# Attention and Fourier mixing on one core: new step lengths, delays, load flows and priorities for a list scheduler

## The chip, the cores and the metric

The kernel runs on one core of a Trainium2 chip. The metric is the device time of one execution in microseconds (us); the time before is the median of three runs. A core has five engines with queues of their own, each strictly in the order in which the program was written: TensorE (PE: matrix products, its weight loads are shown as PEld), VectorE (DVE), ScalarE (ACT), GpSimd (POOL) and SyncE (SP). [...] DMA transfers are issued here from the queues of SP and POOL.

## The reference, cut to what matters

Eight batches, 12 heads, 448 tokens, 64 values per head. Cosine attention first, then a real Fourier mix over tokens and features, a layer norm and a two-layer perceptron of 768, 3072 and 768:

```python
q_n = q / (norm(q) + 1e-6); k_n = k / (norm(k) + 1e-6)
attn = softmax(q_n @ k_n.T / tau)                # tau = 0.1
x = (attn @ v) laid out as [8, 448, 768]
u = x + real(fft(fft(x, axis=1), axis=2))
un = (u - mean(u)) / sqrt(var(u) + 1e-6)
out = u + relu(un @ w_ch1) @ w_ch2
```

## The kernel before, in words

The program is not written in the order in which it runs. `Kern.build` describes every piece of work as a *step* (`Plan.add`): the engines that may run it, a length for each, a priority, a name, and what it reads and writes. `Plan.schedule` then plays the machine through once, on the host while the kernel is built: at each turn it picks, per engine, the step that is ready first (the lower priority number on a tie; ACT and DVE may also wait a little for an urgent step), books it, and moves that engine's clock on. What comes out is nothing but an **order of steps in each of the five queues**, and for copies that ACT or DVE may do, which of them does it. `Plan.emit` writes the instructions in that order with semaphores for every dependency. Lengths and delays decide nothing but a step's place in its queue (and the number of filler groups, below).

Steps have names with a batch number behind the underscore. Those that matter here, with their lines:

- `ld_k`, `ld_q`, `ld_t` (SP) and `ld_v` (POOL, line 847) load queries, keys and values; `W1_n` and `W2_n` (POOL, lines 601 and 602) load twelve blocks of each weight matrix, one behind another three back.
- `sq`, `ss`, `ln`, `nrm`, `eps`, `rcp`, `sc`: squares (ACT, line 677 in batches 0 and 1, 806 later), sums over 64 values (DVE, line 679 or 808), logarithm and exponential for the square root (ACT, lines 620 and 622), reciprocal (DVE, lines 623 and 624), scaling (lines 704, 708 on DVE and POOL in batches 0 and 1, 815 on POOL later).
- Batches 0 and 1 are transposed on PE (`tk`, `tq`, `tt`, lines 732 to 757) and copied out of PSUM by ACT or DVE (line 723; `et` at 767). Batches 2 to 7 are transposed by DMA (`tr`), with two small copies behind it (`ktd`, `qdup`).
- `qk`: scores on PE, 64 rows of the array (line 889), and their tail with 128 rows (`qk?t`, lines 901 and 902). `ex`: exponentials on ACT (line 867). `pv`: values (lines 920 and 926). `rd`, `x`: division on DVE (lines 944 and 946).
- `fa`, `f0`, `f1`, `g` (DVE, lines 963 to 992), `fs` (PE, 1008 and 1013), `te` (1024, 1025), `fd` (PE, 1051), `qe`, `pq`, `u` (1064 to 1079): the two Fourier transforms by folded tables, and the sum u. `sind`, `sinp`, `sinn`, `half` (lines 568 to 586) make the tables while batch 0 runs.
- `ba`, `bs`, `ln2`, `rs`, `un` (lines 1111 to 1120): the layer norm. `tn` (1130) and `eu` (1138) turn batch 0's result; later batches use a DMA transpose (`tru`).
- `h` (line 1188, with `relu` at 1204) is the first product of the perceptron, `y` and `m` (line 1332) the second with its sums (1427) and results (1352 to 1364); for the last two batches `p` (line 1283) takes the place of `h`. These four form the **long stream** of products. Each of its steps depends on the one before (`self.main`), so the order inside the stream is fixed by the code. The scheduler decides only where attention steps of the next batch cut in.

Batch b+1's attention runs between batch b's stream. Before the first `h` (batch 0) there is no stream to fill PE. So `Plan.fill` puts groups of six products that nobody reads (line 1571) into PE's planned gaps of 0.4 us and more, up to the first `h` wherever they fit, later only where PE's planned use is below 0.75.

Priorities are a base (10 + 100 b for attention, 20 more for the Fourier part, 5000 + b for the stream, -1 for what empties PSUM), and a table, `SHIFT`, adds a number to single steps. Delays are constants: 0.11 us from a step to whoever waits for it, 0.2 from PE. `FLOW` has, by name, latency, service time and share of each DMA transfer, and `LATE` an extra reserve behind transfers. The loop at the heart, before:

```python
t = max(t, d.end + (SEM_LAT if d.eng != "pe" else PE_LAT) + (op.late if ... else op.margin if e == "pe" else 0.0))
...
d = op.durs[op.engs.index(e)]
...
op.start = t
free[e] = t + d
op.end = t + d
```

PSUM holds two slots of one bank for the stream and the transposes ("M") and three slots of two banks for attention and mixing ("G").

## Time and profile before

| | us |
|---|---|
| median of three runs (lowest, highest) | 578.48 (577.97, 578.67) |
| span of the profiled execution, first to last instruction | 576.7 |
| PE busy | 562.2 |
| DVE busy | 428.6 |
| ACT busy | 391.4 |
| POOL busy | 210.7 |
| start of the first `h` product | 51.49 |

The time of the profiled execution itself is not given beside its span; the median of the runs is 1.8 us above that span. "Busy" is the time with at least one instruction running. Matmuls overlap in the pipeline, and their ends are modelled: a single product takes some 0.16 us longer to come out than the next one waits to start. So two starts in the timeline, and not a duration, tell what a product costs. In the chain of waits each piece counts only from the end of the piece before, which is why pieces there are shorter than the same instructions in the timeline.

### The profile page before, as it was taken

Reading aid. Unit: us, or ns where it says so; the run is one execution under the profiler, and the core shown is the slowest. Engines: PE = TensorE matmul, PEld = TensorE weight load, DVE = VectorE, ACT = ScalarE, POOL = GpSimd, SP = SyncE. Lnnn points to the kernel's source line nnn. Section 1 sums busy time; section 2 is a strip of 40 time slices with the busy share of each in tenths; the row PEclk is TensorE's granted clock in tenths of the full one; section 3 lists DMA queues with packets and bytes.
Section 4 is the critical chain, followed back from the end, with each engine's and each line's share of the span. In section 5 each row is a group of like instructions: output and inputs, shape, how many; then the busy total and the mean of one; then the engine's idle time right before and its main releaser. Section 6 shows DMA issues by size and latency. Waiting matters only on the chain.

```text
span 576.7 us, 15950 instructions
## 1 busy us (share of the span) xinstructions
PE 562.2 (97%) x6496; PEld 443.3 (77%) x6496; DVE 428.6 (74%) x1066; ACT 391.4 (68%) x764; POOL 210.7 (37%) x323
## 2 busy tenths in 40 slices
PE   3999999999999999999999999999999999999998
PEld 3679888686687786978787687778878687969695
DVE  8879888887688778776768568765877587876363
ACT  8898885467975685687747676488737753848170
POOL 8525424543462525523270435413180120031303
PEclk9899999999999999999999999999999999999999
DMA  9999999892597729952594339932592110022001
GB/s 218 186 218 168 167 180 166 177 166 56 119 150 87 177 44 133 174 110 61 110 140 73 66 103 147 162 70 71 106 108 57 28 57 28 3 42 71 27 30 56
DMA packets 187834, 62.19 MB, mean 108 GB/s; under 512 B 166736, under 2 KB 185552, under 8 KB 187760
## 3 DMA queue, kind: packets, MB, share of 16 engines
q1 hardware_dynamic: 129792, 38.35, 35.2%
q0 software_dynamic: 57968, 22.81, 30.8%
q8 instruction: 51, 0.84, 0.6%
q14 instruction: 23, 0.19, 0.1%
HBM read 51.90 MB, written 11.01 MB: 109 GB/s over the span
## 4 chain that ended last, share of the span: by engine, by line
PE 94%; DVE 3%; POOL 2%; issue 1%; POOLq 0%
PE PS L1332 34%; PE PS L1188 31%; PE PS L1283 7%; PE PS L926 6%; PE PS L889 6%; PE PS L1013 2%; PE PS L920 2%; PE PS L1051 2%; PE PS L744 1%; PE PS L1571 1%; PE PS L901 1%; PE PS L902 1%; POOL VB L847 1%; DVE X L946 1%; DVE SM L679 1%
## 5 line engine op out<-in xcount | busy, mean ns | idle before, releaser
L1188 PE MATMUL PS<-UNT,W1b 128*128 128x256 bf16 (+1 forms) x1872 | 187.9, 256 | 0.0
L1188 PEld LDWEIGHTS PS<-UNT,W1b 128*128 128x128 bf16 x1872 | 156.2, 98 | 18.9 <-issue 4.3
L867 ACT ACTIVATE E<-PS 128x900 bf16<-128x900 f32 (+1 forms) x192 | 148.7, 828 | 27.8 <-PE PS L889 25.7
L1332 PE MATMUL PS<-W2b,HQ 128*128 128x384 bf16 x768 | 133.3, 326 | 0.0
L815 POOL TENSOR_TENSOR QH<-STG,SM 128x256 bf16<-128x256 f32 x126 | 79.1, 655 | 82.1 <-DVE SM L624 73.1
L1332 PEld LDWEIGHTS PS<-W2b,HQ 128*128 128x128 bf16 x768 | 73.9, 98 | 45.4 <-issue 0.9
L1357 POOL TENSOR_TENSOR OUTB<-OUTB,U 128x192 f32<-128x192 f32 x66 | 37.9, 594 | 163.6 <-ACT OUTB L1352 163.3
L1204 ACT ACTIVATE HQ<-PS 128x512 bf16<-128x512 f32 x83 | 49.6, 597 | 42.5 <-PE PS L1188 42.1
L1332 PE MATMUL PS<-TX,HQ 128*128 128x384 bf16 (+2 forms) x408 | 71.0, 321 | 0.0
L1427 DVE TENSOR_TENSOR HQ<-HQ 128x512 bf16<-128x512 bf16 x141 | 60.6, 456 | 13.8 <-ACT HQ L1204 7.7
L1332 PEld LDWEIGHTS PS<-TX,HQ 128*128 128x128 bf16 x408 | 38.4, 98 | 23.5 <-issue 1.1
L926 PE MATMUL PS<-VB,E 128*128 128x65 bf16 x1152 | 51.2, 193 | 0.0
L926 PEld LDWEIGHTS PS<-VB,E 128*128 128x128 bf16 x1152 | 47.6, 97 | 1.1
L806 ACT ACTIVATE QH<-STG 128x384 f32<-128x384 f32 x84 | 42.4, 521 | 7.8 <-DVE SM L808 7.1
L808 DVE TENSOR_REDUCE SM<-QH 128x6 f32<-128x384 f32 x84 | 44.2, 539 | 4.3 <-ACT QH L806 3.9
L1204 DVE TENSOR_SCALAR HQ<-PS 128x512 bf16<-128x512 f32 x43 | 29.7, 691 | 21.1 <-PE PS L1188 20.6
L1386 POOL DMA_INDIRECT out_dram<-OUTB,IDX x21 | 22.9, 1092 | 53.2 <-DVE OUTB L1364 36.4
L920 PE MATMUL PS<-VZ,E 128*128 128x130 bf16 x192 | 41.6, 219 | 0.3 <-DVE X L946 0.3
L889 PE MATMUL PS<-QK 64*128 64x225 bf16 x576 | 39.9, 260 | 0.2 <-ACT E L867 0.2
L1079 DVE SCALAR_TENSOR_TENSOR U<-ACG,X 128x384 bf16<-128x384 f32 (+3 forms) x70 | 39.4, 583 | 0.9
L1352 ACT ACTIVATE OUTB<-PS 128x384 f32<-128x384 f32 x33 | 16.2, 492 | 30.4 <-PE PS L1332 30.1
L946 DVE TENSOR_TENSOR X<-PS,RD 128x512 bf16<-128x512 f32 (+1 forms) x49 | 33.1, 678 | 1.2
(177 smaller groups left out, 795.5 us busy)
## 6 DMA issues: line engine op xcount, KB each, us to landing
STG<-in_k_dram SPq DMA_DIRECT2D x18, 384.0 KB, 4.1
STG<-in_q_dram SPq DMA_DIRECT2D x18, 384.0 KB, 3.8
VB<-in_v_dram POOLq DMA_DIRECT2D x24, 192.0 KB, 5.9
W1b<-in_moe_w_ch_dram POOLq DMA_DIRECT2D x12, 384.0 KB, 6.7
W2b<-in_moe_w_ch_dram POOLq DMA_DIRECT2D x12, 384.0 KB, 7.3
out_dram<-OUTB SPq DMA_DIRECT2D x7, 384.0 KB, 4.0
TX<-in_k_dram SPq DMA_DIRECT2D x2, 576.0 KB, 5.6
TX<-in_q_dram SPq DMA_DIRECT2D x2, 576.0 KB, 6.0
```

The lines of the kernel that those rows point to most:

```text
L806: P.add("act", lambda a, sq=sq, src=buf[:, w * x:w * x + w]: a.activation(sq, src, ACTF.Square), t_act(w), pr, f"sq{i}_{b}", reads=bn, wri ...
L808: P.add("dve", lambda v, o=SS[:, i, H // ns * x:H // ns * (x + 1)], sq=sq: v.tensor_reduce(o, sq.rearrange("p (h d) -> p h d", d=DH), AX.X ...
L815: r = v.tensor_tensor(v3(qh)[:, h:h + 4], v3(buf)[:, h:h + 4], RN[:, i, h:h + 4].unsqueeze(2).to_broadcast((128, 4, DH)), AluOp.mult)
L867: return a.activation(o, self.PS[:, bk:bk + nc_, 0:SQ2], ACTF.Exp, scale=1.0 / self.tau)
L889: i = pe.matmul(self.PS[:, bk + h, c0:c0 + NK], self.KT[r, jj, kt * 128:(kt + 1) * 128], self.QT[r, jj, cols], start=True, stop=True)
L920: r = pe.matmul(o, st(6), self.VZ[:, j, :], start=not split, stop=(split and i == 0), skip_group_check=True)
L926: r = pe.matmul(o[:, 65 * h:65 * h + 65], st(2 * kt + h), self.VB[:, kt, 2 * j + h, :], start=(split and i == h == kt == 0), stop=((not sp ...
L1188: r = pe.matmul(self.PS[:, bk, x * n:(x + 1) * n], self.W1b[:, j, ft * 128:(ft + 1) * 128], self.UNT[:, j, cs], start=(j == 0), stop=(j == ...
L1204: return e.activation(o, i, ACTF.Relu) if e is self.nc.scalar else e.tensor_relu(o, i)
L1283: r = pe.matmul(o[:, 128 * f:128 * f + 128], lhs(j, n * g + f), rhs[:, j, :], start=(start and j == 0 and f == 0), stop=(stop and j == 2 a ...
L1332: r = pe.matmul(self.PS[:, bk, 0:n], lhs(f), rhs(f), start=(start and f == 0), stop=(stop and f == NF // 2 - 1), skip_group_check=True)
L1427: P.add("dve", lambda v: v.tensor_tensor(cs(o), cs(a), cs(bq), op), 0.46, -0.5, f"{nm}{k}_{b}", reads=rd, writes=hr(o)(k))
```

## The change

The steps, their instructions and their dependencies stay. The following becomes different.

- Every step has two lengths from a table `TIMES` (by name and old length): how long until its result counts, and how long it holds its engine. Steps that the table lacks get a rule.
- The delay from a step to its reader is taken by engine, 0.036 to 0.037 us for PE, ACT and DVE and 0.1 for POOL, with 0.018 more when PE is the reader. The extra 0.16 of a product that comes out of PE now stands in its first length.
- `qk` steps (with their tails) are booked 0.095 longer on PE when they follow a step of the long stream.
- `FLOW` has new numbers; the reserves in `LATE` are cut in most places and raised for `h` (0.3 to 0.5).
- `SHIFT` is replaced as a whole: other steps, other numbers, among them for the first time many of the long stream (`h`, `m`, `p`).
- `fill` still asks for gaps of 0.4 us, measured against PE's planned ends, which now are the first of the two lengths.

```diff
-SEM_LAT = 0.11
-PE_LAT = 0.2
+SEM_LAT = {"pe": 0.037, "act": 0.036, "dve": 0.036, "pool": 0.1, "sp": 0.036}
+PE_IN = 0.018
+MODE = 0.095
...
-        r"tru\d_\d": (1.81, 1.0, 0.3), r"tr\d_\d": (1.72, 1.1, 0.38), r"sc_\d_\d": (1.7, 1.56, 0.6), r"st\d_\d": (1.54, 1.0, 1.5)}
+        r"tru\d_\d": (1.81, 1.0, 0.2), r"tr\d_\d": (1.99, 1.23, 0.43), r"sc_\d_\d": (2.12, 1.26, 0.41), r"st\d_\d": (1.26, 1.02, 1.5)}
+
+TIMES = {
+    "pe": {
...
+        "qk0.40": (0.368, 0.300), "qk0.59": (0.562, 0.495), "qk0.78": (0.757, 0.689), "qkt0.20": (0.358, 0.197), "tk0.33": (0.335, 0.174),
...
+        "et0.23": (0.265, 0.289), "et0.29": (0.324, 0.348), "eu0.46": (0.485, 0.371), "ex0.49": (0.546, 0.426), "ex0.83": (0.920, 0.801),
...
 SHIFT = {
-    "cst": {0: 101.5}, "iotad": {0: 116.2}, "vz0": {0: 497.7}, "ix4": {0: -4.5}, "vz1": {0: -249.7}, "pads": {0: 7.3}, "ldt1": {0: -555.5},
...
+    "iotad": {0: 12.9989}, "ktd0": {0: 91.8065}, "vz0": {0: -8.6883}, "vz1": {0: 2.448}, "pads": {0: 2.4458}, "half": {0: -127.0392},
+    "sinn": {0: 78.735}, "ldt": {0: 147.6096}, "ld_q0_0": {0: -17975121.1186}, "ld_t0_0": {0: -17975160.5301}, "sqK0_0": {0: -71.4629},
...
+    "ssT0_1": {0: -209.1662}, "scK0_1": {0: -147.7417}, "scQ0_1": {0: -87.617}, "scK1_1": {0: -147.8435}, "scQ1_1": {0: -78.79},
...
-LATE = {r"W[12]_\d+": 1.5, "tmd": 2.0, r"sq\d_2": 4.0, r"sq\d_\d": 2.0, r"sq[KQT]\d_1": 2.0, r"ktd\d": 3.0, r"qdup\d": 3.0, r"qk\d._[2-7]": 1.5, r"pv\d\d_[2-7]": 2.0, r"pv\d\d_1": 1.0, r"h\d+_[1-7]": 0.3}
+LATE = {r"W[12]_\d+": 1.5, "tmd": 2.0, r"sq\d_\d": 1.5, r"sq[KQT]\d_1": 1.5, r"ktd\d": 2.0, r"qdup\d": 2.0, r"qk\d._[2-7]": 1.5, r"pv\d\d_[2-7]": 1.5, r"pv\d\d_1": 1.0, r"h\d+_[1-7]": 0.5}
...
+        self.mode = 1 if re.match(r"[hymp]\d", name) else 2 if name[:2] == "qk" else 0
+        self.times = {e: self.time(e, d) for e, d in zip(engs, durs)}
+
+    def time(self, e, d):
+
+        key = re.sub(r"\d+", "", re.sub(r"_\d+$", "", self.name)) + f"{d:.2f}"
+        if key in TIMES.get(e, ()):
+            return TIMES[e][key]
+        return {"act": (d + 0.03, max(d - 0.07, 0.05)), "dve": (d + 0.05, max(d - 0.03, 0.05)), "pe": (d + 0.165, d)}.get(e, (d, d))
...
-                    t = max(t, d.end + (SEM_LAT if d.eng != "pe" else PE_LAT) + (op.late if d.dma is not None or d.eng == "pool" and op.late >= 1 else op.margin if e == "pe" else 0.0))
+                    t = max(t, d.end + SEM_LAT[d.eng] + (PE_IN if e == "pe" else 0.0) + (op.late if d.dma is not None or d.eng == "pool" and op.late >= 1 else op.margin if e == "pe" else 0.0))
...
-            d = op.durs[op.engs.index(e)]
+            lat, d = op.times[e]
...
+            if e == "pe":
+                d += MODE * (op.mode == 2 and last == 1)
+                last = op.mode
...
-            op.end = t + d
+            op.end = t + lat + d - op.times[e][1]
```

20 lines of the change are left out of this document (12 added, 8 removed), and 127 rows, old and new, of tables (SHIFT, TIMES).

## The prediction

> **What bounds the kernel now.** I read the page's head first, then the waits of TensorE (PE), then a table of stretches, and last the chain of waits in the start.
>
> ```profile
> span 576.7 us, 15950 instructions
> ## 1 busy us (share of the span) xinstructions
> PE 562.2 (97%) x6496; PEld 443.3 (77%) x6496; DVE 428.6 (74%) x1066; ACT 391.4 (68%) x764; POOL 210.7 (37%) x323
> ```
>
> PE is busy for 97% of the span, so the first question is where the other 3% lie, and whether "busy" hides waits. The waits of PE (engine, line, waited for: total us, times, longest):
>
> ```profile
> PE PS L1571 <- DVE UNT L542: 7.7, 1, 7.7
> PE PS L744 <- POOL TX L704: 0.8, 1, 0.8
> ```
>
> The long one is the wait for the first data. The next longest is 0.8 us, and the view lists none after batch 0's start that is longer. The table of stretches (us; busy time and count of PE, PEld, DVE, ACT, POOL; then granted clock, DMA share, GB/s):
>
> ```profile
> 10.00:20.00 10.00, 8.34 (x81) 6.20 (x79) 8.18 (x18) 8.17 (x16) 7.95 (x12) 0.83 1.64 144
> 16.00:18.00 2.00, 2.00 (x20) 1.44 (x18) 0.61 (x2) 0.93 (x3) 1.45 (x3) 0.50 0.87 35
> 20.00:30.00 10.00, 9.07 (x160) 6.79 (x159) 8.84 (x21) 9.67 (x16) 5.31 (x8) 1.00 1.28 253
> 30.00:40.00 10.00, 9.48 (x173) 7.66 (x170) 7.97 (x23) 9.79 (x13) 1.42 (x2) 1.00 1.30 232
> 40.00:50.00 10.00, 9.08 (x132) 8.44 (x130) 9.11 (x25) 8.98 (x18) 5.68 (x6) 1.00 1.09 138
> 60.00:100.00 40.00, 40.00 (x530) 33.44 (x528) 33.24 (x75) 30.86 (x55) 13.39 (x19) 1.00 1.32 170
> 100.00:200.00 100.00, 100.00 (x931) 73.78 (x929) 79.58 (x203) 69.44 (x149) 47.45 (x69) 1.00 0.77 133
> ```
>
> From 60 us on PE is busy in every stretch, with matmuls that the result needs, and at full clock. ACT (9.67 and 9.79 of 10) sets the pace from 20 to 40: it evaluates batch 0's exponentials (L867). Before 51.5 us, part of PE's busy time is filler (L1571). So two things bound the kernel: **how early the long stream of products starts, and PE's own work after that.** The order of that stream is fixed by a chain of dependencies in the code, which the change leaves alone. It can only be cut up differently by attention steps. The end of the chain of waits that leads to its first product (L1188):
>
> ```profile
> 40.46 1.26 DVE SM L679
> ...
> 43.86 1.01 PE PS L1571 x18
> ...
> 46.99 0.47 DVE QH L708
> ...
> 49.01 0.29 DVE QH L708
> ...
> 51.49 0.55 PE PS L1188 x7
> ```
>
> The three DVE pieces are batch 1's norms and scalings: the first of them reads OUTB, where the code keeps batch 1's squares,
>
> ```profile
> 40.38 1.34 DVE L679 TENSOR_REDUCE SM<-OUTB 128x18 f32<-128x1152 f32 x1
> ```
>
> and all three stand in VectorE's (DVE's) queue ahead of batch 0's mixing. They delay the start of the stream at 51.49.
>
> **The change, term by term.** No instruction is added or removed, except that the number of filler groups follows from the plan. What changes is the order in five queues, and on which of ACT and DVE some copies land. The span is 576.7, and 1.8 lie between it and the median of 578.48. I hold those 1.8 fixed and count against the median.
>
> **(a) Batch 1's steps inside batch 0's last chain.** They cost 1.26 + 0.47 + 0.29 = 2.02 us. The new lengths separate how long a step holds its engine from when its result is visible, so the plan sees this conflict better. Against it speaks the diff: it lifts several of batch 1's steps (`scK0_1` and `scK1_1` by 147.7 from a base of 110) above batch 0's, which have 10 to 32. So more of them may move forward. Bounds: +2.02 gained, or, if the second reduction (the 1.26 again) also lands on the chain, 1.26 lost. I take **1.3 gained**, near the row, less a third that comes back elsewhere.
>
> **(b) The slow stretch ahead of the first scores.** Between 15 and 18 us PE ran at half clock (0.50 in the row 16:18) and filler stands in its queue ahead of the first score products:
>
> ```profile
> 15.11 1.30 PE PS L1571 x12
> 16.41 0.64 PE PS L744 x3
> ```
>
> Eighteen such fillers took 1.01 us at 43.86, so twelve should take 0.67: 0.63 us lie in the way, and behind them waits the first of the exponentials that then fill ACT. Bounds: 0.63 gained, or as much lost if the new plan sets another such group there. I take **0.5 gained**.
>
> **(c) ACT's order in the first norm.** ScalarE's timeline:
>
> ```profile
> 9.27 0.31 ACT L620 ACTIVATE SM<-SM,MV 128x18 f32<-128x18 f32 x1
> 9.60 0.39 ACT L584 ACTIVATE CS<-CS 1x225 bf16<-1x225 bf16 x1
> 10.01 0.22 ACT L622 ACTIVATE SM<-SM 128x18 f32<-128x18 f32 x1
> ```
>
> A table step that nobody needs yet (L584) stands between the logarithm and the exponential of the first norm. It costs 0.39, and a gain of that much is the upper end. The lower end is a loss of the same size, from another table step in its place. The new list moves exactly this step (`half`) and the one behind it (`sinn`). I take **0.4 gained**.
>
> **(d) Cutting up the stream.** The new plan charges 0.095 us when a score step follows a product of the long stream, and nothing when it follows an attention product. PE's timeline shows both cases, first behind the stream, then behind L926:
>
> ```profile
> 256.66 0.38 PE L1188 MATMUL PS<-UNT,W1b 128*128 128x256 bf16 x2
> 256.97 0.76 PE L889 MATMUL PS<-QK 64*128 64x225 bf16 x12
> 257.66 1.48 PE L1188 MATMUL PS<-UNT,W1b 128*128 128x256 bf16 x12
> 258.98 0.26 PE L901 MATMUL PS<-QK,KTD 128*128 128x225 bf16 x1
> ```
>
> ```profile
> 84.45 0.34 PE L926 MATMUL PS<-VB,E 128*128 128x65 bf16 x6
> 84.64 0.22 PE L920 MATMUL PS<-VZ,E 128*128 128x130 bf16 x1
> 84.69 0.34 PE L926 MATMUL PS<-VB,E 128*128 128x65 bf16 x6
> 84.97 0.56 PE L889 MATMUL PS<-QK 64*128 64x225 bf16 x8
> 85.46 0.28 PE L1188 MATMUL PS<-UNT,W1b 128*128 128x256 bf16 x1
> ```
>
> Twelve L1188 of this shape take 258.98 - 257.66 = 1.32, so 0.11 each. The two from 256.66 are through by 256.88, and the score step starts at 256.97: 0.09 lost. Six L926 take 84.64 - 84.45 = 0.19. Those from 84.69 are through by 84.88, and the score step starts at 84.97: 0.09 lost again. So the entry costs the same behind either, and the plan's preference saves nothing. The way out costs too: eight take 0.49 and twelve 0.69, so 0.05 each, and 0.09 are left over. The tail step (L901), of full height, enters at no cost, but the plan charges it as well. After batch 0 the code makes 51 score steps (nine in each of three batches, six in each of four). On paper up to 51 x 0.095 = 4.8 us can be had here; by these rows none. Only two score steps with nothing between them save an exit and an entry, 0.18. Bounds: ten such pairs gain 1.8, ten fewer of those there are now lose 1.8. I take **nothing**, since PSUM slots rarely allow pairs.
>
> [...] By the plan's own rule the forecast would be up to 4.8 us lower.
>
> **Sum:** 1.3 + 0.5 + 0.4 = 2.2 gained; 578.5 - 2.2 = **576.3 us**. What is late next: the last block of the first weights.
>
> ```profile
> 50.69 0.82 POOL L601 DMA_DIRECT2D W1b<-in_moe_w_ch_dram  x1 [2.19 <-DMA W1b<-in_moe_w_ch_dram]
> ```
>
> It leaves at 50.69. Its queue, GpSimd's (POOL's), itself waited 2.19 for an earlier block, so a much earlier stream would run into its weights. The change moves these loads as well (`W1_1` by 143 instead of 0.4, `W1_3` no more by 369), past the value loads on the same queue, and SyncE's (SP's) loads and transposes with them; I see no row that tells the direction. This is why I don't take the full 2.02 + 0.63 + 0.39 = 3.0.
>
> **The rivals.**
>
> *Slower: reserves that were needed.* The new plan cuts the reserve it keeps behind transfers: 3 to 2 us before the copies that follow the transposes (`ktd`, `qdup`), 2 to 1.5 before squares and value products, 4 to 1.5 for batch 2's squares. Every queue is in order. A copy placed too early holds the evictions behind it, these hold PSUM slots, and PE stands.
>
> ```profile
> QK<-QH SPq DMA_TRANSPOSE x42, 3.7
> ```
>
> For it: a transpose takes 3.7 us from issue to landing as a median, so half take longer; and PE has no wait after the start today, so there a new plan can only lose. Against it: the measured flows are longer in part (1.72 to 1.99 for `tr`), so some of the reserve has moved into the lengths. Price: 1.0 us, the cut before `ktd`, in each of the six batches with transposes, 6.0 in all: 576.3 + 6.0 = **582.3**. It decides from 2.2 + 1.2 = 3.4 us on, or 0.57 per batch.
>
> *No change: the plan gains only on paper.* If the new priorities were chosen for term (d), they buy up to 4.8 us that isn't there, and (a) to (c) stay as they are or come back as other intrusions. For it: the diff moves many `h` and `m` steps by about 4600 to 4900, which lifts single products of the stream ahead of attention. Against it: the rows of (a) are plain, and the engine lengths are nearer to the trace. Price: 0 +- 1 us, **578.2**.
>
> *No change: a cold PE at the start of the stream.* Fillers are set into planned gaps of at least 0.4 us, and PE's planned ends now lie 0.16 later, so short gaps lose theirs. If PE idles before 51.49 as it did before 15, the stream starts at half clock. The row 16:18 shows the state, and 10:20 with 0.83 says how long it held: 0.17 of 10 us lost, at half clock, are 3.4 us. Price: half of 3.4, 1.7 us: **578.0**. [...]
>
> **How the numbers follow.** About 0.2% of 578.5, 1.2 us, is what a measurement of this kernel can tell from no change. Chances: forecast 0.55 (its own range 573.6 to 577.3: 3.0 and 1.8 gained at the lower end, 1.2 at the upper), slower by reserves 0.30, plan on paper 0.10, cold PE 0.05. Hence faster 0.55, same 0.15, slower 0.30. The range reaches from 573.0 (the lower end of the likeliest, less most of the 0.7 by which runs differ) to 582.5, the slower rival; some 0.06 lie below it and 0.12 above.
>
> **What would show it.** (a) right: no L679 or L708 in the chain ahead of the first L1188, and that product at about 49.3 instead of 51.49. (b): clock above 0.83 in 10 to 20, first L867 before 17. (c): L622 right behind L620. (d): a score step behind L926 still loses 0.09, and the time from the first L1188 to the end stays within 1 us of 576.7 - 51.5 = 525.2. The slower rival: PE waits after 60 us, for `KTD` copies or exponentials. I am wrong if the first L1188 isn't earlier by over a microsecond, or if the stretch behind it changes by over 2.

## The result and the profile after

The changed kernel takes **582.46 us** (median of four runs, 582.05 to 583.16) against 578.50 of the kernel before (four runs): a ratio of 1.0069, with a 95% interval of 1.0054 to 1.0083. It is 4.0 us slower, at the upper edge of the range, and on the other side than forecast. The profiled execution took 582.19, 1.8 above its span, the same distance as before. In the comparisons further down, 8 of 75 executions of the kernel before took 581.7 to 582.9 us as well, so a ratio there can differ from the quotient of the medians. Every line of the code stands 61 lower than before (L1188 is now L1249).

The page's head, after:

```profile
span 580.4 us, 15813 instructions
## 1 busy us (share of the span) xinstructions
PE 562.0 (97%) x6418; PEld 439.3 (76%) x6418; DVE 434.5 (75%) x1076; ACT 387.5 (67%) x754; POOL 216.1 (37%) x323
```

PE has 78 products fewer, thirteen groups of filler, and is busy as long as before. The span is 3.7 longer. The first product of the long stream says where to cut it: TensorE's timeline of after has it in the last of these rows.

```profile
42.87 0.85 PE L1632 MATMUL PS<-TX 128*128 128x128 bf16 x12 [1.15 <-DVE F L1031]
44.02 0.98 PE L1074 MATMUL PS<-CS,ACG 128*65 128x225 bf16 x8 [0.30 <-DVE ACG L1053]
...
51.08 0.51 PE L1191 MATMUL PS<-TX,F 128*128 128x128 bf16 x6 [0.18 <-DVE F L1181]
...
52.57 0.62 PE L1249 MATMUL PS<-UNT,W1b 128*128 128x128 bf16 x8 [0.35 <-ACT UNT L1199]
```

It starts at 52.57 instead of 51.49: **1.1 of the 3.7 are lost in the start**. The other **2.6 are lost in the stream** (527.8 from there to the end, 525.2 before). I counted them in PE's timeline. A wait is the time from the end of the last product (start plus count times the distance of two starts) to the next product. Waits over 0.25 us come to 3.5 in the stream of after, and before has none: where its useful products stand, at 57.2 and 496.1, it runs 24 products of filler, 1.3 in all, which after doesn't have. Smaller waits make up the other 0.4.

**The start.** The groups of ScalarE between 17 us and the last exponential (count, busy us, mean ns, idle time ahead of them and its releaser), before and then after:

```profile
L867 ACT ACTIVATE E<-PS 128x900 bf16<-128x900 f32 (+1 forms) x24 | 18.4, 832 | 0.2
```

```profile
L928 ACT ACTIVATE E<-PS 128x900 bf16<-128x900 f32 (+1 forms) x24 | 18.1, 837 | 2.2 <-PE PS L950 2.1
```

ACT sets the pace here. Before, it stood 0.2 us ahead of its 24 exponentials; now it stands 2.2, and 2.1 of them wait for scores, 0.6 of it ahead of the first. That first exponential is still 0.7 earlier (16.92 instead of 17.64), but the table load behind the last one is 1.2 later (38.17 instead of 37.01). Why the scores are late shows TensorE's timeline of after, with three transposes of the same shape at three times:

```profile
13.66 0.82 PE L805 MATMUL PS<-TX 128*128 128x128 bf16 x3 [0.31 <-DVE TX L765]
...
16.81 0.82 PE L805 MATMUL PS<-TX 128*128 128x128 bf16 x3
...
19.39 0.55 PE L805 MATMUL PS<-TX 128*128 128x128 bf16 x3
```

Less the 0.16 by which a product comes out later, three take 0.66 until about 19 us, and 0.39 then and 0.33 when warm (0.49 at 26.36). PE runs at half pace while it makes the first scores, as it did before; but before three such transposes were down to 0.54 at 18.29, and here only at 19.39. The table of stretches of after says otherwise:

```profile
10.00:20.00 10.00, 8.33 (x64) 5.40 (x63) 9.54 (x18) 8.37 (x17) 8.77 (x11) 1.00 2.46 151
16.00:18.00 2.00, 2.00 (x16) 1.16 (x15) 2.00 (x4) 1.25 (x2) 1.45 (x3) 1.00 2.97 90
...
60.00:100.00 40.00, 39.41 (x521) 32.35 (x519) 29.44 (x68) 32.19 (x58) 11.67 (x16) 1.00 1.07 156
```

A granted clock of 1.00 at half pace: the trace of after holds no record of the clock at all (its page has no row PEclk, that of before has one), and the column shows 1.00 where nothing is recorded. The lengths of equal products tell the pace here: from one start to the next, the 18 fillers at 19.84 in after take 0.056 each, and the 18 at 52.15 in `before_start` (below) 0.107.

Then two engines meet. VectorE's timeline at the end of batch 0's folding, and GpSimd's, both after:

```profile
41.40 1.75 DVE L1031 TENSOR_TENSOR F<-ACG 128x512 bf16<-128x512 bf16 x2
43.18 0.73 DVE L1584 COPY ACG<-F 128x8 bf16<-128x8 bf16 x1
```

```profile
41.66 2.21 POOL L642 TENSOR_SCALAR CS<-TX 128x770 bf16<-128x770 bf16 x1
```

Before, the same pair took 0.76, and GpSimd's step (`sinp`) began behind it:

```profile
39.70 0.76 DVE L970 TENSOR_TENSOR F<-ACG 128x512 bf16<-128x512 bf16 x2
```

The pair is 1.0 longer, and the copy of eight columns takes 0.73, where 0.19 do without GpSimd (`after_sinp`, below). PE waits 1.15 for the pair (the row at 42.87). The chain of waits behind it holds the batch-1 pieces of term (a):

```profile
43.92 1.10 DVE SM L740
...
45.66 1.72 DVE SM L740 x2
...
49.22 0.94 DVE QH L769 x2
```

They are not gone but longer, 3.76 instead of 2.02. Even so the fold product comes at 44.02 instead of 42.91, and the 8.55 from there to the stream are the 8.58 of before. In this stretch the chain of before shows 2.02 of filler (18 products, twice), but that is no saving of 2.02: behind each group the next product starts 0.2 later than the fillers' pace would have it (from 44.65 to 44.87, from 51.23 to 51.49), so the filler stood in waits that were there anyway. Nor is DVE the only engine with batch-1 work in the way. ScalarE's timeline of after, ahead of the first stream product at 52.57:

```profile
50.98 1.16 ACT L738 ACTIVATE OUTB<-W2b 128x1152 f32<-128x1152 f32 x1
52.03 0.48 ACT L1199 ACTIVATE UNT<-PS 128x384 bf16<-128x384 f32 x1
```

The copy (L1199) for which PE waits could start at 51.59, when the products of the row at 51.08 are out; a square of batch 1 (L738) holds it for 0.4.

**The stream.** TensorE's timeline at its four largest waits behind 53 us, and VectorE's ahead of the third:

```profile
58.61 1.51 PE L1249 MATMUL PS<-UNT,W1b 128*128 128x128 bf16 x24 [0.51 <-DVE TX L1265]
...
73.73 0.22 PE L981 MATMUL PS<-VZ,E 128*128 128x130 bf16 x1 [0.55 <-issue]
...
381.57 1.51 PE L1249 MATMUL PS<-UNT,W1b 128*128 128x128 bf16 x24 [0.57 <-DVE HQ L1265]
...
512.82 3.42 PE L1393 MATMUL PS<-TX,HQ 128*128 128x384 bf16 x20 [0.52 <-DVE HQ L1488]
```

```profile
380.23 0.56 DVE L1140 SCALAR_TENSOR_TENSOR U<-ACG,X 64x384 bf16<-64x384 f32 x1
...
380.83 0.69 DVE L1265 TENSOR_SCALAR HQ<-PS 128x512 bf16<-128x512 f32 x1
```

At 58 and 381 a mixing step (`u`) stands right ahead of the copy (`relu`) that empties the slot PE waits for. At 512 GpSimd is again at work beside DVE: a multiplication ahead of that wait (L1488, at 510.35) takes 0.79, and 0.42 at 377.61 where GpSimd rests. For the wait at 73.73 the profile names no releaser. The other three are no waits for a `KTD` copy or a transpose.

**Theories.** *Lengths*: an order is fitted to the lengths it is planned with. What these have wrong (a cold PE, `sinp` beside DVE, waits that aren't there) becomes gain on paper and loss on the chip. *Reserves*: the cut reserves behind transfers, the slower rival of the prediction. *Start*: all of it comes from the other order of the first 65 us. *Filler*: all of it comes from the fewer groups.

### The profile page after: what moved, and what is told of

It is laid out like the page before. It is cut to its first block, busy times and chain, and to the rows that moved or that the text cites. A ratio compares the mean times of both kernels' runs of the same rounds, so it can differ in the third digit from the quotient of the medians.

```text
span 580.4 us, 15813 instructions
## 1 busy us (share of the span) xinstructions
PE 562.0 (97%) x6418; PEld 439.3 (76%) x6418; DVE 434.5 (75%) x1076; ACT 387.5 (67%) x754; POOL 216.1 (37%) x323
## 4 chain that ended last, share of the span: by engine, by line
PE 86%; DVE 9%; ACT 2%; issue 1%; DMA 1%; SPq 0%; DVEq 0%; ACTq 0%
PE PS L1393 32%; PE PS L1249 27%; PE PS L1344 7%; PE PS L987 6%; PE PS L950 5%; DVE U L1140 3%; PE PS L981 2%; PE PS L1074 2%; PE PS L1112 1%; DMA TX<-in_k_dram 1%; ACT E L928 1%; PE PS L962 1%; PE PS L963 1%; PE PS L805 1%; DVE ACG L1128 1%
## 5 line engine op out<-in xcount | busy, mean ns | idle before, releaser
L1249 PE MATMUL PS<-UNT,W1b 128*128 128x256 bf16 (+1 forms) x1872 | 185.8, 256 | 1.6 <-DVE HQ L1265 0.6
L1249 PEld LDWEIGHTS PS<-UNT,W1b 128*128 128x128 bf16 x1872 | 156.6, 98 | 21.7 <-issue 4.3
L876 POOL TENSOR_TENSOR QH<-STG,SM 128x256 bf16<-128x256 f32 x126 | 83.2, 687 | 80.2 <-DVE SM L685 60.2
L1265 ACT ACTIVATE HQ<-PS 128x512 bf16<-128x512 f32 x88 | 52.5, 596 | 49.1 <-PE PS L1249 48.2
L1488 DVE TENSOR_TENSOR HQ<-HQ 128x512 bf16<-128x512 bf16 x141 | 62.2, 468 | 6.9 <-ACT HQ L1265 4.0
L987 PE MATMUL PS<-VB,E 128*128 128x65 bf16 x1152 | 51.1, 193 | 0.0
L987 PEld LDWEIGHTS PS<-VB,E 128*128 128x128 bf16 x1152 | 47.5, 97 | 1.5
L1140 DVE SCALAR_TENSOR_TENSOR U<-ACG,X 128x384 bf16<-128x384 f32 (+3 forms) x70 | 41.7, 615 | 0.8
L908 POOL DMA_DIRECT2D VB<-in_v_dram x24 | 25.6, 1074 | 43.3 <-PE PS L987 27.5
L1265 DVE TENSOR_SCALAR HQ<-PS 128x512 bf16<-128x512 f32 x38 | 26.2, 690 | 20.6 <-PE PS L1249 20.3
```

The source lines that it names most:

```text
L876: r = v.tensor_tensor(v3(qh)[:, h:h + 4], v3(buf)[:, h:h + 4], RN[:, i, h:h + 4].unsqueeze(2).to_broadcast((128, 4, DH)), AluOp.mult)
L987: r = pe.matmul(o[:, 65 * h:65 * h + 65], st(2 * kt + h), self.VB[:, kt, 2 * j + h, :], start=(split and i == h == kt == 0), stop=((not sp ...
L1140: return v.scalar_tensor_tensor(U[o0:o0 + n, ut, cs].rearrange("p (i e) -> p i e", e=2), src, 1.0, X[i0:i0 + n, x, cs].rearrange("p (i e) ...
L1249: r = pe.matmul(self.PS[:, bk, x * n:(x + 1) * n], self.W1b[:, j, ft * 128:(ft + 1) * 128], self.UNT[:, j, cs], start=(j == 0), stop=(j == ...
L1265: return e.activation(o, i, ACTF.Relu) if e is self.nc.scalar else e.tensor_relu(o, i)
L1488: P.add("dve", lambda v: v.tensor_tensor(cs(o), cs(a), cs(bq), op), 0.46, -0.5, f"{nm}{k}_{b}", reads=rd, writes=hr(o)(k))
```

## The experiments

In kernels with a pinned order a list of steps per queue takes the place of the scheduler's choice, so that only the lines of the diff move. `a_b: 2 -> 1` is the count of filler groups ahead of a step. All ratios are to the kernel before on the same chip.

| kernel | median us | ratio (95%) | first stream product | span less that |
|---|---|---|---|---|
| before | 578.50 | | 51.49 | 525.2 |
| after | 582.46 | 1.0069 (1.0054 to 1.0083) | 52.57 | 527.8 |
| old_start | 581.56 | 1.0028 (1.0006 to 1.0049) | 52.56 | 527.5 |
| new_start | 582.72 | 1.0065 (1.0048 to 1.0082) | 51.74 | 528.8 |
| old_order_new_fill | 580.23 | 1.0031 (1.0011 to 1.0052) | 51.61 | 527.1 |
| prio_only | 645.21 (one run) | | 55.58 | 587.8 |
| after_warm | 582.02 | 1.0061 (1.0048 to 1.0074) | 52.56 | 528.1 |
| after_sinp | 583.07 | 1.0074 (1.0061 to 1.0087) | 52.89 | 528.3 |
| after_evict | 583.80 | 1.0084 (1.0071 to 1.0097) | 53.99 | 528.3 |
| before_warm | 579.68 | 1.0014 (0.9997 to 1.0030) | 51.23 | 526.5 |
| after_dense | 584.21 | 1.0090 (1.0076 to 1.0103) | 52.68 | 530.3 |
| after_mended | 583.55 | 1.0083 (1.0070 to 1.0096) | 51.50 | 529.1 |
| before_start | 582.65 | 1.0059 (1.0046 to 1.0071) | 54.07 | 527.3 |
| after_fix | 582.43 | 1.0056 (1.0041 to 1.0072) | 51.61 | 530.2 |
| hand_84 | 588.41 | 1.0169 (1.0140 to 1.0197) | 56.45 | 530.6 |
| hand_002 | 583.16 | 1.0083 (1.0056 to 1.0110) | 53.51 | 527.9 |
| mode_010 | 584.11 | 1.0115 (1.0076 to 1.0153) | 53.07 | 528.5 |

The last two columns are of each profiled execution. The ratio is that of the comparison on one chip, not the quotient of the medians here.

### Half of the order each, the filler alone, the priorities alone

`old_start`: the queues of before up to 65 us of its plan, then those of after, filler by the new lengths.

```diff
-pe: tq0_0 tk0_0 tt0_0 tk2_0 qk00_0 tq1_0
+pe: tk0_0 tk1_0 tk2_0 tq0_0 tq1_0 qk00_0
...
```

> Every queue keeps the order of the kernel before until batch 0's first pass of up products is through (plan time 65), and has the order of the changed kernel from there. Measured so far: 578.5 before, 582.46 after; PE's useful work in the changed kernel is behind by about 1.0 us at 65 us, 2.2 at 100 and 3.0 at 200. Theory 'start' (the plan mis-sizes batch 0's steps, and what comes later pays for it): 1.0 to 2.2 us come back, 580.3 to 581.5, and the first stream product stands at 51.5 again. Rival 'reserves' (transfers and copies placed too tightly in the later batches): nothing comes back, 582.5 +- 0.6. Rival 'phantom price' (the plan buys 10 cheaper entries of score steps with waits elsewhere in the stream): nothing comes back either, 582.5 +- 0.6.

The time falls by 0.9 by the medians and by more by the ratios (1.0028 instead of 1.0069), but the stream starts at 52.56, no earlier than in after: with the new filler this order is cold too (a granted clock of 0.72 from 10 to 20, 0.83 before). TensorE's timeline shows a wait ahead of the slow products, 1.35 where the kernel before has 0.8, and then two waits of the stream that are those of after:

```profile
15.10 0.80 PE L992 MATMUL PS<-TX 128*128 128x128 bf16 x3 [1.35 <-POOL TX L952]
...
381.12 1.51 PE L1436 MATMUL PS<-UNT,W1b 128*128 128x128 bf16 x24 [0.57 <-DVE HQ L1452]
...
512.51 3.42 PE L1580 MATMUL PS<-TX,HQ 128*128 128x384 bf16 x20 [0.66 <-DVE HQ L1675]
```

So *start* isn't the whole, and the loss in the stream comes with the later order.

`new_start`: the mirror, after's order up to 65 us, then before's, filler by the old lengths (40 groups).

```diff
-pe: tk0_0 tk1_0 tk2_0 tq0_0 tq1_0 qk00_0
+pe: tq0_0 tk0_0 tt0_0 tk2_0 qk00_0 tq1_0
...
```

> The mirror image: the order of the changed kernel until the first up pass is through, then the order of the kernel before. Theory 'start': 1.0 to 2.2 us slower than before, 579.5 to 580.7, and first stream product near 52.6. Rivals 'reserves' and 'phantom price': the time of the kernel before, 578.5 +- 0.6. If old_start and new_start both lie near 582.5, the loss is in neither half but in how they meet.

With the old filler the order of after is warm at 13.5, and ACT stands 1.2 instead of 2.2 ahead of the exponentials:

```profile
L1056 ACT ACTIVATE E<-PS 128x900 bf16<-128x900 f32 (+1 forms) x24 | 17.9, 840 | 1.2 <-PE PS L1078 1.2
```

One of the two microseconds is the cold PE, the other the order itself. The stream starts at 51.74, 0.8 earlier than in after, though the collision is in it too (the pair takes 1.87). What it gains is lost at the seam: batch 1's steps come late for the older rest, and PE waits 2.3 in all from 60 to 76, this one the longest:

```profile
71.58 0.22 PE L1109 MATMUL PS<-VZ,E 128*128 128x130 bf16 x1 [0.63 <-issue]
```

Both mixes lie near 582, so the two halves don't split the loss between them: how the orders meet costs time as well.

`old_order_new_fill`: before's order pinned in all queues, the lengths, delays and flows of after, which here decide the filler alone: 29 groups instead of 37.

```diff
-SEM_LAT = 0.11
-PE_LAT = 0.2
+SEM_LAT = {"pe": 0.037, "act": 0.036, "dve": 0.036, "pool": 0.1, "sp": 0.036}
+PE_IN = 0.018
+MODE = 0.095
...
```

> Order of the kernel before on all five queues; only the filler of PE follows from the new lengths (29 groups in place of 37). Theory 'start' and both rivals: no effect, 578.5 +- 0.6. Theory 'filler' (fewer groups leave PE colder and the clock lower): slower by up to 1.7, the price that the prediction gave to half a stretch at half clock, 580.2, and a granted clock under 1.00 somewhere ahead of 51.5 where the kernel before has 1.00.

1.8 slower by the ratio, but not where *filler* has it: the start loses 0.1. The rest is lost in the stream. There 18 fillers now stand although PE has no gap (1.0), and a wait of 0.75 is new. TensorE's timeline:

```profile
93.77 1.46 PE L1582 MATMUL PS<-W2b,TX 128*128 128x384 bf16 x8 [0.75 <-issue]
...
103.72 1.17 PE L1824 MATMUL PS<-W1b 128*128 128x128 bf16 x18
```

The filler fills a gap that the old order has by the new lengths and not on the chip. That speaks for *lengths*. The wait isn't filler's doing: in this execution a square of ACT waits 2.56 for a load of keys (0.41 in the kernel before), and the copy that PE waits for comes behind it.

`prio_only`: the lengths, delays and flows of before, the priorities of after.

```diff
-SEM_LAT = {"pe": 0.037, "act": 0.036, "dve": 0.036, "pool": 0.1, "sp": 0.036}
-PE_IN = 0.018
-MODE = 0.095
+SEM_LAT = 0.11
+PE_LAT = 0.2
...
```

> The scheduler of the kernel before with its one length per step, and only the new list of priorities. The list was made for the new lengths. If priorities carry over by themselves, the time is that of one of the two kernels, 578 to 583. If a list fits only the lengths that it was made with, queues run into one another: I expect over 600.

645.21 us, a span of 643.4: 67 us more than the kernel before. But most of it is filler. The page:

```profile
L1577 PE MATMUL PS<-W1b 128*128 128x128 bf16 x1020 | 61.4, 219 | 0.2
```

With the old lengths the new list leaves gaps in the plan, and 170 groups of filler go into the stream: 1020 products at 0.056 are 57 of the 62.6 by which the stream is longer. How much of that covers waits that the chip would have shown, this run doesn't tell. So the list doesn't carry over to other lengths, but 67 us is not the price of its order alone.

### Mending after's start and its waits

`after_warm`: six more filler groups ahead of the first transposes.

```diff
-tq0_0: 7, tk0_0: 0, tk2_0: 0
+tq0_0: 9, tk0_0: 3, tk2_0: 1
```

> The changed kernel with all its orders, and 6 more groups of filler on PE ahead of batch 0's first transposes (9 in place of 7 ahead of the first one, 3 and 1 ahead of two later ones). In the changed kernel's trace PE runs at about 0.6 of its pace until 19.4 us (three products 0.82 us, 0.55 from there on), in new_start, with these groups, at full pace from 13.5 on. Theory 'cold start' (24 groups in place of 37 leave PE slow ahead of the scores): full pace from about 13.5, first product of the stream at 51.7 instead of 52.57, and 0.8 off the end, 581.6; if the chain behind gives some back, 581.6 to 582.3. Rival 'the start is set by the queues alone' (order): no effect, 582.46 +- 0.4.

PE is warm, ACT stands 1.2 only, and useful products are 1.4 ahead of after at 40 us. The collision and what follows it take it all. TensorE's timeline:

```profile
41.87 0.51 PE L1826 MATMUL PS<-TX 128*128 128x128 bf16 x6 [1.53 <-DVE F L1222]
...
43.17 1.71 PE L1265 MATMUL PS<-CS,ACG 128*65 128x225 bf16 x8
```

PE stands for 1.53 and, behind six fillers at full pace, for another 0.29; then eight products take 1.71 instead of 0.98 (the row at 44.02 of after): half pace again, and the clock record of this trace has it too, 0.5 from 42.81 to 46.22. The stream starts at 52.56, and the time is that of after.

`after_sinp`: GpSimd's step beside the pair (`sinp`) goes to DVE, behind the fold.

```diff
-pool: W1_6 W1_8 sinp W1_7
+pool: W1_6 W1_8 W1_7
-dve: g1_0:0 g1_0:1
+dve: g1_0:0 g1_0:1 sinp
```

> The changed kernel with one step moved: the sine table step that GpSimd computes from 41.66 to 43.9 us goes to DVE, behind the last of the fold's sums (g1). In the changed kernel the fold's pair of sums took 1.75 us beside it, 0.76 in the kernel before. Theory 'two engines slow each other': the pair takes 0.76 again, the step itself costs DVE 0.5 or so, the first product comes 0.5 earlier, 52.1, the end 581.9. Rival 'the pair was slow for another reason': it stays at 1.75, the first product comes 0.5 later, the end at 583.

VectorE's timeline:

```profile
42.28 0.76 DVE L1222 TENSOR_TENSOR F<-ACG 128x512 bf16<-128x512 bf16 x2
43.08 0.19 DVE L1775 COPY ACG<-F 128x8 bf16<-128x8 bf16 x1
...
43.57 0.52 DVE L833 TENSOR_SCALAR CS<-TX 128x770 bf16<-128x770 bf16 x1
```

The pair is back at 0.76 and the copy at 0.19, and the step that took GpSimd 2.21 takes DVE 0.52. That the collision is GpSimd's doing is shown. Yet PE stayed cold longer in this execution (ACT stood 3.0 ahead of the exponentials), the pair begins 0.9 later than in after, and the time is 0.6 above it. How the two hinder each other is not shown. In after the pair was done at 43.15, ahead of the end of GpSimd's step at 43.87 (GpSimd's ends are rough), so by these rows it didn't wait for the whole of that step.

`after_evict`: three copies out of PSUM ahead of the `u` steps, where three of the four waits stood.

```diff
-dve: u1_0:4 u1_0:2 relu8_0 | relu16_4:1 behind u1_5:5 | s21_6 behind s40_6
+dve: relu8_0 u1_0:4 u1_0:2 | relu16_4:1 behind u1_5:3 | s21_6 behind s22_6
```

> The changed kernel with three copies on DVE moved ahead of three mixing steps (u) that stand before them, where its trace shows PE waiting for those copies: at 58.6 (0.67 us), 381.6 (0.74) and 512.8 (0.68). Theory 'evictions behind u steps' (the u steps take 0.6 a piece where the table has 0.48): the three waits go, 2.1 in all, 580.4; if a product waits for the delayed u step instead, half of it, 581.4. Rival 'reserves': these waits only show what a late transfer left, others take their place, 582.46 +- 0.4.

The wait at 381 shrinks from 0.57 to 0.26 and the one at 512 is gone, so those were rightly read. The first moved copy gives 0.7 back from 60 to 70, and PE was cold until 22 in this execution: 18 fillers at 20 us took 2.08, and 1.17 in after with the same order. The start is 1.4 later, which no moved line explains.

`after_dense` and `after_mended`: filler groups that wait for DVE steps 1.6 us earlier and are more (38), alone, and with `sinp` on DVE and two of the three moved copies.

```diff
-tq0_0: 7, fs0_0: 2, fs1_0: 2, fd0_0: 2, tk0_1: 2, h0_0: 1
+tq0_0: 9, tk0_0: 3, tk2_0: 1, fs0_0: 3, fs1_0: 6, fd0_0: 3, tk0_1: 3, h0_0: 2
-new.deps.add([o for o in self.order["dve"] if o.end + 0.05 <= at + 0.1][-1])
+new.deps.add([o for o in self.order["dve"] if o.end + 0.05 <= at - 1.5][-1])
```

> The changed kernel with all its orders and 38 groups of filler in place of 24, in the start alone: as in after_warm, and 4 more ahead of the second fold's products (there after_warm stood 1.53 us, and its 8 products took 1.71 behind that, 0.98 in new_start), 1 more each ahead of the first fold, the mixing products, batch 1's first transpose and the stream. The fillers also wait for DVE steps that end 1.6 us earlier, so that none is held by a late one. Theory 'cold start': PE at full pace from 13.5 us to the stream without a break, 8 products in 0.98, first stream product at 51.6, end 0.9 earlier than the changed kernel, 581.5. Rival 'queues alone': first stream product between 52.3 and 52.6, end 582.0 to 582.5.

> after_dense with two more edits: the sine step on DVE in place of GpSimd (in after_sinp it freed the fold's pair of sums, 0.76 in place of 1.75), and the two late copies ahead of mixing steps (in after_evict the waits at 381 and 512 us went from 0.57 and 0.52 to 0.26 and 0). If all three count and nothing is given back: 0.9 + 0.5 + 0.8 = 2.2 below the changed kernel, 580.3. If the start has slack behind it (what PE gains ahead of the stream is lost at the first step of batch 1 that comes late): 0.8 + 0.3, 581.4.

`after_dense`: the early groups are through too soon, PE waits 2.2 behind them and is slow again (18 fillers in 1.76); the stream starts at 52.68. `after_mended` has the same steps and filler up to 40 us and waits 2.96 there, but PE stays at full pace (18 fillers in 1.17): between these two, part of the gain is the execution's and not the edit's. Its stream starts at 51.50, as in before, and useful products are 1.0 to 1.4 us ahead of after until 300 us. Then TensorE's timeline, and ScalarE's and the queue of SP with its transposes:

```profile
302.28 1.49 PE L1440 MATMUL PS<-UNT,W1b 128*128 128x256 bf16 x12 [0.54 <-ACT HQ L1456]
```

```profile
301.22 0.52 ACT L1058 ACTIVATE QH<-STG 128x384 f32<-128x384 f32 x1 [0.92 <-DMA QK<-QH]
```

```profile
293.58 6.12 SPq L1073 DMA_TRANSPOSE QK<-QH  x4
```

A square of a later batch waits 0.92 for a transpose; the copy behind it on ACT is late, and PE stands 0.54. In `after_dense` the same chain costs 1.43 at 304.44. In after the four transposes take 5.42 and nobody waits. This is the mechanism of *reserves*, real, but only 0.5 to 1.4 us, and only where other edits made PE earlier. After itself doesn't pay it.

`after_fix`: the filler, `sinp` on DVE, all three copies with the first on ACT, and that square later.

```diff
 (after_mended's edits; filler waits 1.6 earlier only behind 35 us)
-dve: u1_0:4 relu8_0 u1_0:2      act: relu12_3:1 sq0_6:1 sq6_5 (relu2_3:1 behind)
+act: bs1_0 relu8_0              act: sq0_6:1 relu2_3:1 sq6_5
```

> The changed kernel with its late steps put right one by one: the fillers of after_warm and after_dense (those ahead of 35 us timed as in after_warm), the sine step on DVE, the copies that PE waited for at 381 and 512 us ahead of mixing steps, the one at 58 us (relu8) moved from DVE, where it stands behind three mixing steps, to ACT, which has 1.2 and 0.7 us free there, and the square on ACT that waited for a transpose in after_mended and after_dense (at 300 us, 0.9 and 1.8) behind the copy that it held up. In the changed kernel PE's waits over 0.25 us from the first stream product on add up to 3.5 us, 0.5 in the kernel before. Theory 'late copies' (the stream loses its time in single waits for copies and exponentials that the plan puts too close): first stream product at 51.3 to 51.6, waits over 0.25 us at 1.5 or less, end 582.46 - 1.1 - 1.9 = 579.5. Rival 'given back' (each repair lets PE run into the next late step): waits stay at 3 or more, end 582 to 584, as after_mended.

The stream starts at 51.61 and the mended waits are gone (0.26 is left behind 381), but others of the same size stand elsewhere. TensorE's timeline, the two largest:

```profile
59.43 0.50 PE L997 MATMUL PS<-TX 128*128 128x128 bf16 x3 [0.72 <-DVE TX L957]
...
304.37 0.98 PE L1266 MATMUL PS<-CS,ACG 128*65 128x225 bf16 x8 [0.92 <-DVE ACG L1245]
```

582.43, after's time: 1.0 gained in the start is given back in the stream, as *given back* has it. (Counted from start to start, the kernel before has no wait over 0.25 us in its stream, not 0.5.) No mended version beats the kernel before.

### The prediction's terms on the kernel before

`before_warm`: term (b) alone; the filler ahead of the first scores goes to earlier places.

```diff
-tq1_0: 2, tk2_0: 1, tq0_0: 0
+tq1_0: 0, tk2_0: 2, tq0_0: 2
```

> Term (b) of the prediction alone, on the kernel before: the 12 fillers ahead of the second query transpose go, 18 more stand in the gap ahead of the first one, where PE waits 0.8 us for GpSimd. All orders are those of the kernel before. By term (b): full pace from 14.6 on, first scores at 16.4 instead of 17.04, first stream product 0.5 earlier (51.0), end 0.5 earlier, 578.2 beside 578.7. Rival 'the exponentials take their pace from elsewhere': first scores earlier, but first stream product within 0.2 of 51.49 and the end unchanged. Rival 'the start has slack': the stream starts 0.5 earlier, and PE waits that much later on, at 496 or before; end unchanged.

Everything is 0.61 earlier up to the fold, just what the term said. Then VectorE's and GpSimd's timelines:

```profile
41.03 1.80 DVE L1185 TENSOR_TENSOR ACG<-F 128x256 bf16<-128x256 bf16 x2
```

```profile
41.80 2.21 POOL L774 TENSOR_SCALAR CS<-TX 128x770 bf16<-128x770 bf16 x1
```

GpSimd's step stands behind a load in its queue and comes at 41.80 instead of 42.51, as much earlier as DVE: this pair takes 1.80, where it took 1.12 before. The 1.12 seem not to be free of it either. VectorE's timeline of before, and of `before_start`, where DVE does that step:

```profile
41.64 1.12 DVE L992 TENSOR_TENSOR ACG<-F 128x256 bf16<-128x256 bf16 x2
```

```profile
40.90 0.51 DVE L1246 TENSOR_TENSOR ACG<-F 128x256 bf16<-128x256 bf16 x2
```

So the kernel before probably paid 0.6 already, though GpSimd's step is shown to begin late in the pair (its times are rough). The fold product comes at 42.88 instead of 42.91. The ratio can't be told from 1.

`before_start`: terms (a) and (c); batch 1's reductions and scalings behind batch 0's mixing, batch 0's steps ahead on ACT, `sinp` on DVE.

```diff
-dve: f11_0 ssK0_1 ... scK1_1 scK2_1 un0_0
+dve: g1_0:1 sinp te1_0:1 ssK0_1 u0_0:0 u0_0:1 ... un0_0 scK1_1 scK2_1
-pool: W1_8 sinp
-pe: fd1_0:0 tk0_1 fd1_0:1 tk1_1 tk2_1 tn0_0
+pe: fd1_0:0 fd1_0:1 tk0_1 tn0_0 tk1_1 ... h3_0 tk2_1
-act: sind gc1_0 ... sqT0_1 te0_0 te1_0 ... ek1_1 ek2_1 eu00_0 eu01_0
+act: sind te0_0 gc1_0 te1_0 ... rs0_0 eu00_0 eu01_0 ... ek1_1 ek2_1
```

> The kernel before with batch 0's last chain cleared as terms (a) and (c) of the prediction wanted it: on DVE the first reduction of batch 1's squares (1.26 us at 40.46) goes behind the copy that follows the second fold, two scalings of 0.47 behind the normalisation of the first tile, and the sine step comes to DVE behind the fold's sums; on ACT the two copies of the mixed keys and the small copy stand ahead of the table load (1.28) in place of behind it; three transposes of batch 1 on PE and their copies stand later. By the prediction's step (a): first stream product 1.3 to 2.0 earlier than 51.49, end 1.3 to 2.0 earlier, 576.8 to 577.5. Rival 'given back': first stream product 1 to 2 earlier, but batch 1's steps, now later, hold PE after 55 us for as long, end 578.5 to 579.5. Rival 'another gate': the mixing products wait for something else, first stream product within 0.5 of 51.49.

The fold product is 0.43 earlier and the mixing 0.57. Then ACT is the gate, in the chain of waits:

```profile
46.25 1.05 ACT W2b L931
47.30 1.05 ACT OUTB L931
```

Two squares of batch 1 stand ahead of batch 0's normalisation on ACT. PE waits 1.85 for it, the next products run at half pace (18 fillers in 2.13), and the stream starts at 54.07. So the 2.02 of term (a) are not to be had from DVE alone: another engine with batch-1 work is late next.

### Are the lengths it? Other numbers, planned anew

If one length is short, another number should let the plan come true. `hand_84` plans with a longer delay into PE, `hand_002` and `mode_010` with nearly the same numbers.

```diff
-PE_IN = 0.018
+PE_IN = 0.084
```

```diff
-PE_IN = 0.018
+PE_IN = 0.020
```

```diff
-MODE = 0.095
+MODE = 0.100
```

> The changed kernel with one number changed: the planner reckons 0.084 us in place of 0.018 for PE to take up work that another engine hands over, so 0.12 per hand-over in all, about what the kernel before reckoned (0.11); the planner orders all five queues anew by it. Its plan ends at 582.5 us, that of the changed kernel at 575.2 (measured span 580.4, so 5.2 later than planned), that of the kernel before at 582.1 (576.7, 5.4 earlier than planned). Theory 'reserve' (the waits of the stream come from hand-overs planned without reserve): PE's waits over 0.25 us from the first stream product on fall from 3.5 to 1 or less, and the span lies near the plan or below, 579 to 583, time 581 to 585. Rival 'lengths' (each step is late by its own error, reserve or not): waits stay at 3 or more, span 5 above the plan, time near 589.

> As hand_84, with 0.020 in place of 0.018: next to no change of the lengths, but the planner orders anew; plan end 575.9. Theory 'picked by the plan' (the list of priorities was chosen for the end of its own plan, so that plan ends too early by what the model leaves out, 5.2 us): span 581.1 +- 1, time 582.9 +- 1. If a chance order is as good as the picked one by the chip, but not by the plan, the time lies within 1 of 582.5 as well, and the planned end says nothing about the last 1%.

> As hand_002, with the price of a score step behind the stream at 0.100 in place of 0.095 and the hand-over as in the changed kernel; plan end 577.0. Theory 'picked by the plan': span 582.2 +- 1, time 584 +- 1. The start, which the plan leaves as it was, gives the same first stream product as the changed kernel, 52.6 +- 0.4, and PE's waits over 0.25 us in the stream lie at 3 or more again.

(`hand_84` doesn't compute the reference's result, and why is open. All its products run; its time is that of an order that can't be used.)

The spans are 587.0, 581.4 and 581.6 where the scheduler's own ends are 582.5, 575.9 and 577.0: later by 4.5, 5.5 and 4.6, and 4.0 to 4.4 of it are lost before the stream starts. A longer delay into PE only adds its own time (waits over 0.25 us in the stream are 5.9 instead of 3.5), so what is missing isn't a delay of this kind. The change of 0.002 us moves 34 steps of the first three batches, and the profiled execution starts its stream 0.9 later than after; that of 0.005 moves 577 steps, none of them of batch 0. The medians are 0.7 and 1.7 above after's, the first no clear difference. The bands of *picked by the plan* hold both spans, but for `hand_002` its alternative holds as well, so that is not decided; `hand_84` came out as *lengths* had it.

What the kernel's scheduler books for the two orders (filler takes no time in it) stands beside the chip's spans so:

| order | lengths | stream starts | stream lasts | end |
|---|---|---|---|---|
| before's | old, on paper | 52.6 | 529.5 | 582.1 |
| before's | new, on paper | 49.9 | 531.5 | 581.4 |
| before's | chip | 51.5 | 525.2 | 576.7 |
| after's | new, on paper | 48.7 | 526.4 | 575.1 |
| after's | chip | 52.6 | 527.8 | 580.4 |

By its own lengths the change gains 6.2 us, 1.2 in the start and 5.1 in the stream. The chip gives -1.1 and -2.6. In the old order's stream the new lengths book 3.6 us of waits over 0.25 us, of which the chip shows none in the kernel before (filler of 1.3 covers two places). The new order has 0.6 of them on paper, and 3.5 on the chip. So the new priorities **avoid waits that weren't there, and buy for it waits that the lengths don't show**. The start is too short on paper for both orders, by 1.6 for the old and by 3.9 for the new.

## Why the prediction was wrong

**The sum** missed by 6.2 us (576.3, and 582.46): it had 2.2 gained ahead of the stream, where 1.1 were lost, and nothing behind its first product, where 2.6 were lost. **The bound** was rightly named: how early the stream starts, and PE's own work after that. Both tests that I set for being wrong came true: the first stream product is later, not earlier by a microsecond, and the stretch behind it is 2.6 longer.

**(a), 1.3 gained: wrong sign.** The step that failed reads "I take 1.3 gained, near the row". The batch-1 pieces on the chain grew from 2.02 to 3.76. I had the evidence against me (the diff lifts `scK0_1` and `scK1_1`), and gave it no weight against a plain row. And the 2.02 were no free money: `before_start` shows ACT's batch-1 squares as the next gate. I counted the path to the stream on DVE, without asking what ACT still had to do; in after, too, a batch-1 square stands ahead of ACT's last copy.

**(b), 0.5 gained: no gain.** The filler ahead of the first scores cost what I said, as `before_warm` shows (0.61). What failed is the cover: I named the weights as what is late next, and it was `sinp` on GpSimd: DVE, 0.6 earlier, loses 0.7 more beside it. In after the term fell differently: with 24 filler groups for 37 PE stays at half pace a microsecond longer, and ACT waits 2.2. My sign for it, a clock over 0.83 from 10 to 20, reads 1.00 only because nothing is recorded, and meant nothing.

**(c), 0.4 gained: no gain.** The step moved as foreseen. ScalarE's timeline of after:

```profile
10.20 0.39 ACT L645 ACTIVATE CS<-CS 1x225 bf16<-1x225 bf16 x1
10.62 0.32 ACT L681 ACTIVATE SM<-SM,MV 128x24 f32<-128x24 f32 x1
10.84 1.15 ACT L738 ACTIVATE HQ<-TX 128x1152 f32<-128x1152 f32 x1
```

`half` (L645) is out from between logarithm and exponential, and a square of 1.15 is in. The lower end that I kept (another table step) was too small: what may come in is any step of the engine.

**(d), nothing: right for the entries, wrong for the stream.** TensorE's timeline of after, behind the stream:

```profile
255.84 7.37 PE L1249 MATMUL PS<-UNT,W1b 128*128 128x256 bf16 x66
263.14 0.76 PE L950 MATMUL PS<-QK 64*128 64x225 bf16 x12
```

The 66 are through at 255.84 + 66 x 0.1093 = 263.05, so 0.09 are lost again. Over the whole kernel 49 score steps enter behind the stream before, at 0.095 as a mean. After, it is 39 at 0.101, and ten others enter behind attention products (7 behind L987 at 0.094, 3 behind L963 at 0.101). Ten entries were moved, and none was saved. (One of the 39 holds a wait of 0.21; without it their mean is 0.096.) But (d) was also the only term for the stream, and that its other waits would stay as they were had no reason beside it: 3.5 us of new waits came, the largest part of the loss.

**The rivals.** *Reserves* gave 582.3 and a chance of 0.30, and the time was 582.46: right in sign and size, wrong in mechanism. None of after's large waits with a named releaser is for a transpose or a `KTD` copy. The size is luck. The mechanism appears in `after_dense` and `after_mended`, with 1.4 and 0.5 instead of 6. *Plan on paper* (0.10) was nearest in kind: 6.2 us gained there, and not for term (d), which is worth ten entries or 0.95. But I took "on paper" to end at no change, and it ended at a loss. *Cold PE at the stream's start* (0.05) had the right state at the wrong place: it costs at the first scores, 1.0 us of ACT's 2.2.

**What was missing** is a rival of its own: lengths that are off where the old order is good make the new priorities trade a good order for a worse one. Its price could have been bounded by the rows of before: PE had no wait over 0.25 us and 1.3 us of filler in the whole stream, so there was next to nothing to win behind 51.5 but the entries of (d), and those I had at nothing.

**Shown**: the collision (`after_sinp`, `before_warm`), the cold PE (`after_warm`, `new_start`), the late copies at 381 and 512 (`after_evict`), filler without a gap (`old_order_new_fill`). **Only argued**: that the wrong lengths are why the new order is worse, from the table of plans, and that priorities fitted to better lengths would do better; none were made, and no mended version won the time back. The scheduler does hold DVE beside GpSimd for some steps (`PIECE`), and `sinp` isn't among them. **Open**: which single lengths make the old order's stream 6.3 too long on paper, and which are short in the start beyond the cold PE and the collision.

## What to carry to other kernels

A list of priorities found with one cost model is part of that model: before it is fitted to new lengths, plan the old order with them and hold it against the chip, for what they have wrong there is what the fit will chase. A microsecond taken out of a chain is worth it only up to the next engine whose work stays where it was, so look at what runs beside the earlier step (here GpSimd, then ACT) before the sum is made. Count filler by what stands around it: in a wait that is there anyway it costs nothing (in before the product behind 18 fillers starts 0.2 later than their pace would have it), without one it costs its own length (1.0 us in `old_order_new_fill`). And read PE's pace from equal products; the clock column shows 1.00 where nothing is recorded.

## What the runs showed of the hardware

- A trace can lack the record of the clock: in after the column reads 1.00 throughout, while three equal transposes take 0.82 at 16.81 and 0.49 at 26.36. In `after_warm`, whose trace has the record, 0.5 from 42.81 to 46.22 goes with eight products in 1.71 instead of 0.98.
- How long PE stays slow differs between executions of the same order of products: 18 fillers at 20 us took 1.17 in after, 1.58 in `after_sinp` and 2.08 in `after_evict`.
- The length of one wait doesn't tell whether half pace follows: it did behind waits of 1.53 and 0.29 (`after_warm`, 41.87 and 42.66) and of 2.23 (`after_dense`, 13.91), and did not behind 2.96 (`after_mended`, 13.95).
- One GpSimd step over 770 columns beside DVE: two steps of 512 columns in 1.75 (after) and 1.87 (`new_start`) instead of 0.76 (before, `after_sinp`), two of 256 in 1.80 (`before_warm`) instead of 0.51 (`before_start`), a copy of eight columns in 0.73 (after) instead of 0.19 (`after_sinp`). The step itself takes GpSimd 2.21 (after) and DVE 0.36 (`before_start`) and 0.52 (`after_sinp`).
- The same four transposes took 5.42 (after), 6.12 (`after_mended`) and 6.47 us (`after_dense`) from issue to landing.
